# Output tiles 0 and 3 of the first batch pair computed as one group of seven products, with the output-weight sums in another order

## The chip, the core and the metric

The kernel runs on one core of a Trainium2 chip, as one program. The time is the device time of one execution in microseconds (us). A core has five engines that are used here: TensorE (PE; PEld is its weight load), VectorE (DVE), ScalarE (ACT), GpSimd (POOL) and SyncE (SP, which here only starts transfers). Each runs its own list of instructions in order, and they wait for one another through semaphores.

## What is computed

Eight batches of twelve heads, 448 positions and 64 elements go through an attention with a sigmoid in place of the softmax, and the result (3584 tokens of 768) through a gated feed-forward block:

```python
scores = scale * np.matmul(q, k.transpose(0, 1, 3, 2)) - np.log(S)
attn = 1.0 / (1.0 + np.exp(-scores))
x = np.matmul(attn, v)                  # heads side by side: 3584 x 768
g = x @ w_gate                          # 768 x 1536
out = (g * sigmoid(g) * (x @ w_val)) @ w_out      # 1536 x 768
```

## The kernel before

**Tiling.** Work goes in four pairs of batches (`pb` 0 to 3, batches 2·pb and 2·pb+1). The hidden layer has 1536 columns, in twelve blocks `f` of 128. For a batch `b` and a block `f`, `ffn1` (matmuls on line 314) multiplies x by the gate and value weights, twelve matmuls of 448 columns. Its gate follows: a sigmoid on ACT (line 334) and two products on DVE (336, 340), the last of which writes `hT`, the hidden block. Blocks 0 to 5 of pair 2 and all of pair 3 (`FAST`) are computed by `double` instead (matmuls on line 437, evictions by ACT on line 447 and DVE on line 460 and after), which takes two blocks of both batches at once with seven products instead of eight. Pair 2 runs its `ffn1` blocks 6 to 11 first and its `double` units after them.

**Output.** The 896 tokens of a pair are seven output tiles of 128 tokens (`m` 0 to 6). There are two ways to compute them:

- `ffn2` (matmuls on line 675) does one tile alone: twelve blocks by two halves of 384 columns, 24 matmuls. ACT evicts the first half (line 690) and DVE the second (line 689).
- `ffn2_group(pb, g)` (line 599) does tiles g and g+3 together, as a 2 by 2 block product with seven products of six matmuls instead of eight, 42 in place of 48. The products run in the order 1, 2, 6, 5, 7, 3, 4 and use the two banks of one PSUM tile in turn: 1, 6, 7 and 4 go to bank 0, and 2, 5 and 3 to bank 1. Before the next product may write or add to a bank, what is in it has been read by DVE (`snap`, line 610, and `put`, line 616), or for the first product by ACT (line 623) where the argument `act` is set.

The group needs sums. `make_sums` (line 532) forms sums of hidden blocks on DVE. `w_sum(s, kind)` (line 498) forms sums of the output weights, once for the whole kernel: eight DVE operations of 128 by 1152, for two halves `s` of the blocks and four kinds. Kind 2 is made from kind 3 and kind 4 from kind 2. Product 6 uses kind 2, product 5 kind 1, product 7 kind 3 and product 4 kind 4; products 1, 2 and 3 use the plain weights.

**PSUM.** It is a ring of four tiles of two banks each. Every user (`Banked`) takes the next of the four, in turn: one for each scores tile, each P·V result, each `ffn1` unit, each `ffn2` and each group. So a user always writes over the tile of the user four places before it, bank by bank, and has to wait until each bank has been read there.

**Order.** A list `units` holds the feed-forward work in order, each with an estimated duration (`FU1` 2.26 for an `ffn1`, `FU2` 3.9 for an `ffn2`, `FU3` 6.83 for a group); sums have 0. The attention is cut into `visits` of three or four score tiles (scores on line 240, their sigmoid on ACT line 259 or 256), and P·V of a finished head group (line 273, copies on DVE lines 288 and 293, or ACT line 301) follows in a later visit. Every visit has a due time, read off the line of points `PACE` over the estimated time. A loop adds up the durations of the units and puts a visit ahead of the first unit whose start is past the due time:

```python
    PACE = ((2 * NJ, FIRST + 3.5), (3 * NJ, FIRST + 41.5), (3 * NJ + 2, FIRST + 60.5), (6 * NJ, f1_end[B - 5] - 1.0), (NQ, f1_end[B - 3] - 5.0))
```

`f1_end[b]` is the estimated end of batch b's `ffn1` blocks, and contains the durations of the output units of earlier pairs. So the estimates of the first pair's output units also set where later visits go. The P·V of the last visit is done after the next `ffn1` unit; if the next unit is a `double`, it is done right ahead of that.

**First pair's output before the change.** In the list it was: all hidden sums; `ffn2` of tile 6; `w_sum` (0,3) (0,2) (0,1) (0,4); `ffn2` of tile 0; `w_sum` (1,3) (1,2) (1,1); `ffn2` of tile 3; group 1 (tiles 1 and 4), during which `w_sum` (1,4) is made; group 2 (tiles 2 and 5). The attention visits lie between them.

Of the kernel before, what the change touches and what calls it, by code (L numbers as in the profile page):

```python
# [20 lines left out]
def kernel(  # L21
# [22 lines left out]
    LAST = B // 2 - 1  # L44
# [99 lines left out]
    def half_of(a):  # L144
        return a.rearrange("p a b s -> p (a b s)").bitcast(FP16)
# [212 lines left out]
    def fast_w(s, kind, i=None):  # L358

        js = slice(0, JT) if i is None else slice(i, i + 1)  # L360
        b11, b21 = wg16[s][:, 0::2][:, js], wg16[s][:, 1::2][:, js]
        b12, b22 = wv16[s][:, 0::2][:, js], wv16[s][:, 1::2][:, js]
        if (s, kind) not in gT:
            n = JT * FW * 128
            at = {3: 0, 2: 1, 4: 2}.get(kind)
            if kind == 1:
                t = wv16[s][:, 0::2]
            elif s == 0:
                t = half_of(stg_a)[:, at * n:(at + 1) * n]
            elif s == 1 and kind == 3:  # L370
                t = half_of(ramp_a)[:, 8 * FW * hw:8 * FW * hw + n]
            elif s == 1:
                t = pt_f[:, (at - 1) * n:at * n]
            elif s == 2:
                t = pt_f[:, (at + 2) * n:(at + 3) * n]
            else:
                t = osp.tile([128, DM], FP32, tag="osb", name=f"g{kind}").bitcast(FP16)[:, :n]
            gT[(s, kind)] = t if kind == 1 else t.rearrange("p (j n) -> p j n", j=JT)
        t = gT[(s, kind)][:, js]
        a, b, op = {  # L380
            3: (b22, b12, SUB), 1: (b12, b11, SUB), 2: (b22, gT.get((s, 1), gT[(s, kind)])[:, js], SUB),
            4: (b21, gT.get((s, 2), gT[(s, kind)])[:, js], SUB),
        }[kind]
        (V if i is None else G).tensor_tensor(out=t, in0=a, in1=b, op=op)
# [104 lines left out]
    def w_sum(s, kind):  # L489

        b11, b12 = wo16[2 * s][:, :, :hw], wo16[2 * s][:, :, hw:]
        b21, b22 = wo16[2 * s + 1][:, :, :hw], wo16[2 * s + 1][:, :, hw:]
        t = half_of(ramp_a)[:, len(wT) * FW * hw:(len(wT) + 1) * FW * hw].rearrange("p (f n) -> p f n", f=FW)
        wT[(kind, s)] = t
        a, b, op = {
            3: (b22, b12, SUB), 2: (wT.get((3, s)), b11, ADD), 1: (b12, b11, SUB), 4: (b21, wT.get((2, s)), SUB),
        }[kind]
        nc.vector.tensor_tensor(out=t, in0=a, in1=b, op=op)
# [158 lines left out]
        store((nc.sync, nc.scalar), *rows[1], oe, lo)  # L657

    def ffn2_groups(pb, gs, extra=()):
        gens = [ffn2_group(pb, g, len(gs) > 1) for g in gs]  # L660
        extra = list(extra)
        while gens:
            gens = [g for g in gens if next(g, g) is not g]
            if extra:
                extra.pop(0)()
# [30 lines left out]
    FU1, FU2, FU3, FU4 = 2.26, 3.9, 6.83, 7.85  # L696
# [3 lines left out]
    for pb in range(B // 2):  # L700
        for b in (2 * pb, 2 * pb + 1):
            f1_start[b] = tt
            for f in range(NF):
                if f not in FAST.get(pb, ()):
                    if b or f > 2:
                        units.append((FU1, ffn1, (b, f)))
                    tt += FU1
            f1_end[b] = tt
        for f in FAST.get(pb, ())[::2]:
            extra = {  # L710
                (LAST - 1, 0): ((0, 4), (1, 2)), (LAST - 1, 2): ((1, 4),), (LAST, 0): ((3, 3), (3, 1)), (LAST, 2): ((3, 2), (3, 4)),
            }.get((pb, f), ())
            units.append((FU4, double, (pb, (f, f + 1), [lambda a=a: fast_w(*a) for a in extra])))
            tt += FU4
        o_units = [(0.0, make_sums, (99,))]
        if pb < LAST - 1:
            o_units.append((FU2, ffn2, (pb, C - 1)))
        if pb == 0:

            ts = [(0.0, w_sum, (s, kind)) for s in range(2) for kind in (3, 2, 1, 4)]  # L720
            o_units += ts[:4] + [(FU2, ffn2, (pb, 0))] + ts[4:7] + [(FU2, ffn2, (pb, 3))]
        ex = {(0, 1): (lambda: None, lambda: w_sum(1, 4)), (LAST - 1, 0): (keep_rest,)}
        gs = {0: ((1,), (2,)), LAST - 1: ((0, 1), (2,)), LAST: ((0, 1), (3,), (2,))}.get(pb, ((0,), (1,), (2,)))
        for g in gs:
            o_units.append((FU3 * len(g), ffn2_groups, (pb, g, ex.get((pb, g[0]), ()))))
        units += o_units
        tt += sum(u[0] for u in o_units)
# [142 lines left out]
    early = [tile_of(0), tile_of(2)]  # L870
# [126 lines left out]
```

## Time and profile before

| | us |
|---|---|
| median of 4 runs | 404.38 |
| lowest and highest | 403.76, 405.43 |
| the profiled execution, its own time | 404.66 |
| its span, first to last instruction | 402.9 |

| engine | busy us | share of the span |
|---|---|---|
| PE | 391.5 | 97% |
| DVE | 269.5 | 67% |
| ACT | 230.3 | 57% |
| POOL | 104.9 | 26% |

The span is the time between the first and the last instruction on the core; 1.76 us of the execution's time lie around it. The granted clock of TensorE was 0.998 of full speed. In a timeline row, the columns are the start, the length, the engine, the line and operation, what is written and read (without buffer numbers), and in brackets the engine's idle time before it with what ended it; rows of the same line that follow one another are merged and counted (x3). In the chain of waits, each row is a start, a length, an engine and a line: the work that the end of the program goes back to.

### The profile page before, as it was taken

The page shows a single profiled execution, that of the slowest core. Times are in us where ns is not written, and L with a number is a line of the kernel's source. Part 1 is how long each engine was busy: PE and PEld are TensorE (multiplying, and loading weights), DVE is VectorE, ACT ScalarE, POOL GpSimd, SP SyncE. Part 2 cuts the span into 40 slices and gives each one's busy share as a digit, 9 for nine tenths or more (in the row PEclk, how much of TensorE's full clock was granted, in tenths as well). Part 3 has the DMA queues.
Part 4 walks back from the last instruction along what each step waited for, and adds up shares of the span by engine and source line. Part 5 has one row for each costly group of instructions (what it writes and reads, how often), then busy time and mean ns, then how long its engine had stood idle before and what let it go on. Part 6 is the DMA issues. An engine that isn't in the chain of part 4 may idle for free.

```text
span 402.9 us, 8032 instructions
## 1 busy us (share of the span) xinstructions
PE 391.5 (97%) x3134; PEld 203.9 (51%) x3134; DVE 269.5 (67%) x509; ACT 230.3 (57%) x369; POOL 104.9 (26%) x146
## 2 busy tenths in 40 slices
PE   7799999999999999999999999999999999999995
PEld 3344544545555444444455554444555655555663
DVE  2637657779765555567774556788877578778753
ACT  5965885744344777777773447776654055756000
POOL 4528031333121232321310210000006970010700
PEclk9999999999999999999999999999999999999999
DMA  8999989999859998778716598000000520000055
GB/s 273 245 248 253 245 187 232 174 167 218 150 160 261 215 234 218 163 159 161 161 23 130 165 260 135 2 2 0 3 0 2 157 80 0 1 2 1 2 164 149
DMA packets 65286, 54.39 MB, mean 135 GB/s; under 512 B 35744, under 2 KB 61440, under 8 KB 65248
## 3 DMA queue, kind: packets, MB, share of 16 engines
q1 hardware_dynamic: 49744, 38.22, 38.5%
q0 software_dynamic: 15072, 15.34, 22.7%
q8 instruction: 24, 0.39, 0.4%
q10 hardware_dynamic: 432, 0.33, 0.3%
q14 instruction: 14, 0.11, 0.1%
HBM read 47.19 MB, written 11.01 MB: 144 GB/s over the span
## 4 chain that ended last, share of the span: by engine, by line
PE 93%; DVE 3%; ACT 2%; issue 1%; DVEq 0%; ACTq 0%
PE ps_D L314 33%; PE ps_D L599 20%; PE ps_D L437 18%; PE ps_D L240 8%; PE ps_D L273 8%; PE ps_D L675 4%; ACT pt_a L259 2%; PE ps_D L769 1%; PE ps_D L210 1%; DVE S L532 1%; DVE t L336 1%; DVE T L216 0%; ACT s L334 0%; DVE hT L340 0%; DVE xT L293 0%
## 5 line engine op out<-in xcount | busy, mean ns | idle before, releaser
L259 ACT ACTIVATE pt_a<-ps_D 128x896 f16<-128x896 f32 x148 | 127.1, 919 | 55.5 <-PE ps_D L240 50.1
L314 PE MATMUL ps_D<-xT,wg 128*128 128x448 f16 x360 | 79.4, 353 | 0.6 <-DVE t L336 0.5
L314 PE MATMUL ps_D<-xT,wv 128*128 128x448 f16 x360 | 78.9, 352 | 0.0
L191 POOL CAST c<-stg_a 128x896 bf16<-128x896 f32 x40 | 37.1, 937 | 132.8 <-DMA stg_a<-in_q_dram 116.9
L336 DVE TENSOR_TENSOR t<-ps_D,s 128x448 f16<-128x448 f32 x60 | 37.4, 623 | 43.0 <-ACT s L334 42.0
L314 PEld LDWEIGHTS <-wg 128*128 128x128 f16 x360 | 32.3, 98 | 39.4 <-issue 13.6
L314 PEld LDWEIGHTS <-wv 128*128 128x128 f16 x360 | 35.1, 98 | 33.0 <-issue 0.4
L334 ACT ACTIVATE s<-ps_D 128x448 f16<-128x448 f32 x60 | 33.1, 551 | 26.5 <-PE ps_D L314 26.5
L240 PE MATMUL ps_D<-T,T 64*64 64x448 bf16 x644 | 44.2, 357 | 2.2 <-DVE T L216 1.2
L447 ACT ACTIVATE snap<-ps_D 128x448 f32<-128x448 f32 x54 | 28.0, 541 | 26.7 <-PE ps_D L437 25.1
L340 DVE SCALAR_TENSOR_TENSOR hT<-ps_D,t 128x448 f16<-128x448 f32 x60 | 37.5, 625 | 6.3
L273 PE MATMUL ps_D<-pt_a,v 64*64 64x448 f16 x672 | 36.0, 350 | 1.3 <-DVE hT L340 0.7
L610 DVE TENSOR_SCALAR osb<-ps_D 128x384 f32<-128x384 f32 x43 | 23.9, 557 | 18.6 <-PE ps_D L599 17.9
L599 PEld LDWEIGHTS <-S 128*128 128x128 f16 x264 | 25.8, 98 | 17.1
L599 PE MATMUL ps_D<-ramp_a,S 128*128 128x384 f16 x198 | 33.6, 326 | 0.0
L616 DVE SCALAR_TENSOR_TENSOR osb<-ps_D,osb 128x384 f32<-128x384 f32 x36 | 19.9, 556 | 13.8 <-PE ps_D L599 13.8
L240 PEld LDWEIGHTS <-T 64*64 64x64 bf16 x644 | 14.9, 105 | 24.5 <-issue 17.9
L599 PEld LDWEIGHTS <-hT 128*128 128x128 f16 x204 | 19.6, 98 | 14.5 <-issue 1.8
L273 PEld LDWEIGHTS <-v 64*64 64x64 f16 x672 | 19.5, 107 | 14.2 <-issue 1.7
L288 DVE CAST xT<-ps_D 128x448 f16<-128x448 f32 x21 | 13.1, 623 | 19.3 <-PE ps_D L273 17.5
L293 DVE CAST xT<-ps_D 64x448 f16<-64x448 f32 x37 | 23.0, 622 | 0.8
L437 PE MATMUL ps_D<-xS,wv 128*128 128x448 f16 x108 | 23.4, 352 | 0.0
(110 smaller groups left out, 443.5 us busy)
## 6 DMA issues: line engine op xcount, KB each, us to landing
out_dram<-osb SPq DMA_DIRECT2D x52, 192.0 KB, 3.2
stg_a<-in_q_dram SPq DMA_DIRECT2D x18, 448.0 KB, 5.1
stg_a<-in_k_dram SPq DMA_DIRECT2D x18, 448.0 KB, 5.6
v<-in_v_dram POOLq DMA_DIRECT2D x24, 224.0 KB, 5.9
wg<-in_moe_w_gate_dram POOLq DMA_DIRECT2D x4, 576.0 KB, 12.0
wv<-in_moe_w_val_dram POOLq DMA_DIRECT2D x4, 576.0 KB, 13.1
wo<-in_moe_w_out_dram POOLq DMA_DIRECT2D x4, 576.0 KB, 9.7
stg_a<-in_q_dram POOLq DMA_DIRECT2D x3, 448.0 KB, 14.0
```

Source lines behind the costliest of these rows:

```text
L191: eng.tensor_copy(out=t.rearrange("p c h d -> p h c d"), in_=st.rearrange("p h (c d) -> p h c d", c=C))
L240: nc.tensor.matmul(out=sc[w * 64:(w + 1) * 64, h2, :S], lhsT=kt[r, w * 64:(w + 1) * 64], rhs=qt[r, :, w * 64:(w + 1) * 64], start=True, st ...
L259: nc.scalar.activation(out=pt, in_=sc[:, :, :S], func=SIGM, bias=sbias, scale=qkscale)
L273: nc.tensor.matmul(out=P[g:g + 64, h2, :S], lhsT=vt[r, h2, c * D:(c + 1) * D], rhs=pt[r, h2, :], start=(c == 0), stop=(c == C - 1),)
L314: nc.tensor.matmul(out=D.t[:, i, :S], lhsT=(wg16, wv16)[i][f // FW][:, pr, cs], rhs=xT[(b, pr)], start=(pr == 0), stop=(pr == NP - 1),),
L334: D.read(nc.scalar.activation(out=s16, in_=D.t[:, 0, :S], func=SIGM), 0)
L336: D.read(nc.vector.tensor_tensor(out=t1, in0=D.t[:, 0, :S], in1=s16, op=MULT), 0)
L340: nc.vector.scalar_tensor_tensor(out=hT[(b // 2, f)][:, b % 2, :], in0=D.t[:, 1, :S], scalar=hsc(b // 2), in1=t1, op0=MULT, op1=MULT),
L437: nc.tensor.matmul(out=D.t[:, bank, :S], lhsT=W(f, j), rhs=X(j), start=(start and j == 0), stop=(stop and j == JT - 1), skip_group_check=True,
L447: D.read(nc.scalar.mul(out=o, in_=D.t[:, bank, :S], mul=scale), bank)
L599: nc.tensor.matmul(out=D.t[:, bank, :hw], lhsT=l, rhs=B_(i), start=(first and i == 0), stop=(i == HF - 1), skip_group_check=True,),
L610: nc.vector.tensor_scalar(out=o, in0=D.t[:, bank, :hw], scalar1=1.0 / hsc(pb), scalar2=None, op0=MULT), bank
```

## The change

Tiles 0 and 3 of pair 0 become group 0, `ffn2_group(0, 0)`, with the first product read by ACT. Of the sums of the output weights, four now stand ahead of tile 6's `ffn2`: (0,3) (0,2) (1,3) (1,2). Two, (0,1) and (1,1), stand between that and group 0. The two of kind 4 are made inside group 0, after its third and its fourth step (product 6 and product 5). Group 1 no longer makes a sum. The estimated duration of the first pair's output falls from 3·3.9 + 2·6.83 = 25.36 to 3.9 + 3·6.83 = 24.39.

```diff
     def ffn2_groups(pb, gs, extra=()):
-        gens = [ffn2_group(pb, g, len(gs) > 1) for g in gs]
+        gens = [ffn2_group(pb, g, len(gs) > 1 or (pb, g) == (0, 0)) for g in gs]
...
         if pb < LAST - 1:
             o_units.append((FU2, ffn2, (pb, C - 1)))
         if pb == 0:
-
-            ts = [(0.0, w_sum, (s, kind)) for s in range(2) for kind in (3, 2, 1, 4)]
-            o_units += ts[:4] + [(FU2, ffn2, (pb, 0))] + ts[4:7] + [(FU2, ffn2, (pb, 3))]
-        ex = {(0, 1): (lambda: None, lambda: w_sum(1, 4)), (LAST - 1, 0): (keep_rest,)}
-        gs = {0: ((1,), (2,)), LAST - 1: ((0, 1), (2,)), LAST: ((0, 1), (3,), (2,))}.get(pb, ((0,), (1,), (2,)))
+            early = [(0.0, w_sum, a) for a in ((0, 3), (0, 2), (1, 3), (1, 2), (0, 1), (1, 1))]
+            o_units[1:1] = early[:4]
+            o_units += early[4:]
+        skip = lambda: None
+        ex = {
+            (0, 0): (skip, skip, lambda: w_sum(0, 4), lambda: w_sum(1, 4)), (LAST - 1, 0): (keep_rest,),
+        }
+        gs = {LAST - 1: ((0, 1), (2,)), LAST: ((0, 1), (3,), (2,))}.get(pb, ((0,), (1,), (2,)))
```

## The prediction

> **What bounds the kernel.** I read the page's busy shares and chain first, then the chain in order of time around the output of pair 0 and around the last visit, then DVE's and ACT's timelines there.
>
> ```profile
> PE 391.5 (97%) x3134; PEld 203.9 (51%) x3134; DVE 269.5 (67%) x509; ACT 230.3 (57%) x369; POOL 104.9 (26%) x146
> PE 93%; DVE 3%; ACT 2%; issue 1%; DVEq 0%; ACTq 0%
> ```
>
> ```profile
> 98.10 3.90 PE ps_D L675 x24
> 102.00 0.69 PE ps_D L240 x12
> 102.70 7.91 PE ps_D L675 x48
> 110.60 0.50 PE ps_D L240 x8
> ...
> 272.38 0.69 PE ps_D L240 x12
> 273.07 2.38 PE ps_D L314 x12
> 275.44 1.45 PE ps_D L273 x28
> 276.89 2.38 PE ps_D L314 x12
> 279.27 23.84 PE ps_D L437 x126
> ```
>
> From 95 us on PE is back to back: each piece starts where the last one ends, and no other engine stands between. So a matmul less is worth its time, and a wait that PE gets is lost in full, since nothing later has idle time to give back.
>
> ```profile
> 98.65 0.62 DVE L340 SCALAR_TENSOR_TENSOR hT<-ps_D,t 128x448 f16<-128x448 f32 x1
> ...
> 101.98 0.62 DVE L532 TENSOR_TENSOR S<-hT,S 128x384 f16<-128x384 f16 x2
> 102.51 0.55 DVE L689 TENSOR_SCALAR osb<-ps_D 128x384 f32<-128x384 f32 x1
> 102.98 0.75 DVE L498 TENSOR_TENSOR ramp_a<-wo,wo 128x1152 f16<-128x1152 f16 x1
> 103.76 0.76 DVE L498 TENSOR_TENSOR ramp_a<-ramp_a,wo 128x1152 f16<-128x1152 f16 x1
> 104.44 0.75 DVE L498 TENSOR_TENSOR ramp_a<-wo 128x1152 f16<-128x1152 f16 x1
> 105.11 0.75 DVE L498 TENSOR_TENSOR ramp_a<-wo,ramp_a 128x1152 f16<-128x1152 f16 x1
> ```
>
> DVE isn't idle between 98.65 and 105.86. Tile 6's eviction (L689) comes as soon as the hidden sums (L532) are done, and the weight sums (L498) follow it.
>
> ```profile
> 102.37 2.54 ACT L259 ACTIVATE pt_a<-ps_D 128x896 f16<-128x896 f32 x3
> ...
> 272.74 2.54 ACT L259 ACTIVATE pt_a<-ps_D 128x896 f16<-128x896 f32 x3 [0.72 <-PE ps_D L240]
> 272.78 0.62 DVE L340 SCALAR_TENSOR_TENSOR hT<-ps_D,t 128x448 f16<-128x448 f32 x1
> ```
>
> The three sigmoids of a visit take ACT until 2.54 us after the first starts, 0.36 us after the visit's scores began at 272.38.
>
> **The matmuls.** 48 matmuls in 7.91 us are 0.165 us each; the chain has a whole group of 42 at 112.81 in 6.93. Six fewer: **-0.98**.
>
> **The moved sums and the ring.** Ring users after the change are tile 6's `ffn2`, three score tiles, then group 0: group 0 writes tile 6's PSUM tile. Its product 1 (bank 0) waits for ACT's L690, done by 102.37, which costs nothing. Product 2 (bank 1) waits for DVE's L689. This now stands behind four L498. Hidden sums end at 101.98+0.62 = 102.60; the four take about what they take before, 105.86-102.98 = 2.88, so to 105.5; L689 ends about 106.08. Product 1 runs 102.70 to 103.68, product 2 from 106.12: a wait of **2.44**. Behind L689 on DVE are everything that releases the group's banks, and on SP tile 6's store with the transposes of head group 10 and a load behind it, which go 3 us later than at 104.39; head group 10 isn't read before 127, so that is covered.
>
> The rest of the group, in steps of 0.98, an eviction of 0.56 that can start some 0.2 after its product's last matmul has issued, and L498 of 0.75:
> - DVE does (0,1) and (1,1) to 107.43, the put of product 2 to 107.99. PE does product 2 to 107.10 and 6 to 108.07 (ACT's eviction of product 1 follows the sigmoids, 104.91+0.5 = 105.4; that would be a wait of 0.75 if the first weren't there). Product 5 needs the put: just in time.
> - DVE evicts 6 by 108.83, sums (0,4) by 109.52, evicts 5 by 110.06, sums (1,4) by 110.75, puts 7 by 111.3. PE does 5 to 109.05, 7 to 110.02, waits 0.06, 3 to 111.08, waits for the put of 7: **0.26**; product 4 ends at 112.32.
>
> Group 0 thus ends at 112.32 where 48 matmuls ended at 110.60: **+1.72** in all, with the 0.98 gained counted. The following visit's third score tile takes the group's PSUM tile at 114.1, after the last eviction (113.1).
>
> Bounds. Two hidden sums there took 1.07 and 1.11 where the others take 0.35, beside POOL casts at 99.12 and 100.26. If those casts land elsewhere, DVE is 1.47 earlier; product 2 starts at 104.65, but product 5 then waits for its put, to 106.6, and the group ends near 110.75, **+0.2**. If as many other sums are hit as well it is 1.47 worse, **+3.2**. POOL has no work between 102.0 and 110.6, so I keep 1.7.
>
> The Trainium skill's page "TensorE: Matmul & The Clock Gate" (Part 1) bears on such a wait. In the trace, PE was busy for only 2.78 of the 4.00 us from 8 to 12 with the clock at 1.00. By the page, an idle window of about 3.4 us halves the clock for about as long; 2.44 is below it. By the rule the sum stays as it is; were the wait just above the window it would be an estimated 1.7 dearer. No row here shows such an idle window.
>
> **The estimate and the visits.** The first pair's estimate falls by 0.97, and so does that of `f1_end[5]`, the last point of `PACE`. In the built order the visits keep their places up to the end of pair 1; from there each comes one `ffn1` unit, or one output unit, later. In most places that only swaps blocks of PE work: I go through DVE's queue in pair 2 and the copies of P·V end just before the next visit's first score tile needs them (by 272.2 where PE comes at 272.3). That is cost nothing, with 0.1 of cover.
>
> At the end it does cost. The last visit now stands right before `double`. Its P·V has no `ffn1` unit ahead of it, and needs the visit's last sigmoid. In the times of before, with scores from 272.38: P·V's PSUM tile is that of the preceding `ffn1`, free when L340 ends at 273.40 (there it may be 0.1 later, with one more hidden sum ahead). Sixteen of its matmuls run to 274.2; the last sigmoid ends at 275.28, the last four matmuls (0.19) at 275.5. `double` starts there, 3.13 after the scores. The two units that stood between are done earlier, at 4.64 for two in a row (chain: 4.64 or 4.65). Sum 3.13+4.64 = 7.77; before, 279.27-272.38 = 6.89: **+0.88**. The bounds: 0.1 more or less by the DVE order, and 0.3 less if the first sigmoid starts sooner. `double`'s own evictions are later against it by about 0.3, as the activation table load now follows the last sigmoid; the next use of that bank comes 0.7 after them, so nothing.
>
> **Sum.** 1.72 + 0.88 = 2.6. On the profiled execution: 404.66 + 2.6 = 407.3; it was 0.28 over the median 404.38, so the median goes to **407.0**.
>
> **Rivals.**
> - *Both as worked out*: 406.1 to 408.0 (group 0 from +1.2 to +2.6, end from +0.5 to +1.0). 66%.
> - *The saving stands (not slower)*: L689 gets through early, because DVE has reached the sums sooner, and group 0 runs without a wait. Price: -0.98, with the end's +0.88 then 404.3, without it 403.4. It decides where L689 ends by 103.7, before product 2; this needs the four L498 (2.88) to start at 100.3, where DVE still has four hidden sums to do. The 67% of DVE speaks for it, the rows above against it. 10%, nearly all of it within 0.3%.
> - *The end costs nothing*: +1.7 alone, 406.1; if the last sigmoids come before P·V's matmuls do. Against: ACT has 2.54 for them, PE 1.5 of work. 14%, from 405.7 to 406.4.
> - *More*: a store or a transpose behind L689 on SP becomes late, or DVE is held up by casts in group 0 also, and PE waits 1.5 to 2 more: 408.0 to 409. For it: only 0.1 of cover in pair 2. 10%.
>
> 0.3% is 1.2 us, about what a measurement of this kernel can tell from no change. Faster by over that has 3% (it needs -1.2, more than all six matmuls), same 9%, slower 88%. The range leaves out most of the second rival and half of the last: 405.5 to 408.6.
>
> **What would show it.** In the chain of the changed kernel, DVE L498 and L689 between the scores at 102.0 and group 0's matmuls; L689 near 105.5; group 0 (L599 x42) over about 9.6 us instead of 6.9. At the end ACT L259 in the chain, between the scores and P·V, right ahead of L437; the other groups at 6.93. I am wrong if product 2 starts right after product 1, if the group's 42 matmuls take 7 us, or if P·V before L437 takes 1.3 as elsewhere.

## The result

The changed kernel takes 405.98 us, the median of 50 runs (405.20 to 411.34), where the kernel before takes 404.54 on the same chips (74 runs). The ratio is 1.0036, with a 95% interval of 1.0025 to 1.0046: 1.0 to 1.9 us slower. The forecast of 407.0 had the sign right and was 1.0 us too high; its range held the time. The profiled execution of after took 405.97 (span 404.2), 1.31 more than that of before.

From the page of after, the busy shares and the chain's shares:

```profile
PE 393.2 (97%) x3128; PEld 204.9 (51%) x3128; DVE 272.5 (67%) x514; ACT 229.5 (57%) x367; POOL 105.7 (26%) x146
PE 30%; ACT 0%; DVE 0%; issue 0%; DVEq 0%
```

PE has six matmuls less, and DVE is busy for 3.0 more. The chain gives PE 30% only because it could not be followed back beyond 279.23 us. So stages are compared here by their start times in the timelines instead. Three marks serve for every kernel: the scores of the visit ahead of the output that is in question (L240 x12, at 101.93 in before) to the scores behind it; from those to the first matmul of the first `double` after the last visit (L437); from there to the last eviction (L610). In before's timelines these are

```profile
101.93 0.76 PE L240 MATMUL ps_D<-T,T 64*64 64x448 bf16 x12
110.53 0.57 PE L240 MATMUL ps_D<-T,T 64*64 64x448 bf16 x8
279.11 2.43 PE L437 MATMUL ps_D<-xT,wg 128*128 128x448 f16 x12
398.66 0.56 DVE L610 TENSOR_SCALAR stg_a<-ps_D 128x384 f32<-128x384 f32 x1 [0.49 <-PE ps_D L599]
```

and in after's the last two (the first two are the first and the last row of group 0's timeline further down)

```profile
280.41 2.44 PE L437 MATMUL ps_D<-xT,wg 128*128 128x448 f16 x12
399.97 0.56 DVE L610 TENSOR_SCALAR stg_a<-ps_D 128x384 f32<-128x384 f32 x1 [0.49 <-PE ps_D L599]
```

| kernel | scores to scores | to `double` | to the last eviction | sum |
|---|---|---|---|---|
| before | 8.60 | 168.58 | 119.55 | 296.73 |
| after | 8.59 | 170.04 | 119.56 | 298.19 |

The sum rises by 1.46; the first scores came 0.15 sooner in after's execution, which leaves the 1.31. So the group of seven products takes as long as the two tiles alone took, though it has six matmuls less, and the whole loss lies at the end.

Group 0, in PE's and DVE's timelines of after (start, length, engine, line, operation; the brackets tell what ended the idle time):

```profile
101.78 0.76 PE L240 MATMUL ps_D<-T,T 64*64 64x448 bf16 x12
102.48 1.15 PE L599 MATMUL ps_D<-wo,hT 128*128 128x384 f16 x6
104.28 1.14 PE L599 MATMUL ps_D<-wo,hT 128*128 128x384 f16 x6 [0.66 <-DVE osb L689]
105.25 3.09 PE L599 MATMUL ps_D<-ramp_a,S 128*128 128x384 f16 x18
108.18 1.14 PE L599 MATMUL ps_D<-wo,S 128*128 128x384 f16 x6
109.30 1.14 PE L599 MATMUL ps_D<-ramp_a,hT 128*128 128x384 f16 x6
110.37 0.57 PE L240 MATMUL ps_D<-T,T 64*64 64x448 bf16 x8
```

```profile
99.94 0.36 DVE L532 TENSOR_TENSOR S<-S,hT 128x384 f16<-128x384 f16 x1
100.22 0.62 DVE L532 TENSOR_TENSOR S<-hT,S 128x384 f16<-128x384 f16 x2
100.76 0.75 DVE L498 TENSOR_TENSOR ramp_a<-wo,wo 128x1152 f16<-128x1152 f16 x1
101.54 0.76 DVE L498 TENSOR_TENSOR ramp_a<-ramp_a,wo 128x1152 f16<-128x1152 f16 x1
102.22 0.75 DVE L498 TENSOR_TENSOR ramp_a<-wo,wo 128x1152 f16<-128x1152 f16 x1
103.00 0.76 DVE L498 TENSOR_TENSOR ramp_a<-ramp_a,wo 128x1152 f16<-128x1152 f16 x1
103.68 0.55 DVE L689 TENSOR_SCALAR osb<-ps_D 128x384 f32<-128x384 f32 x1
```

Product 2 waits for tile 6's eviction L689, and this is behind the four L498, as forecast. But the wait is 0.66 and not 2.44, as the hidden sums (L532) take 0.36 and less here and the four weight sums begin at 100.76. The forecast had counted its 2.44 from start to start, less the step of 0.98; counted like that the wait is 0.82 (104.28 - 102.48 - 0.98).

The end, in after's timeline:

```profile
274.45 0.75 DVE L384 TENSOR_TENSOR stg_a<-wv 128x1152 f16<-128x1152 f16 x1
275.12 0.62 DVE L288 CAST stg_a<-ps_D 128x448 f16<-128x448 f32 x1
275.77 1.26 DVE L293 CAST stg_a<-ps_D 64x448 f16<-64x448 f32 x2
277.08 0.76 PE L240 MATMUL ps_D<-T,T 64*64 64x448 bf16 x12 [0.32 <-DVE stg_a L293]
277.51 2.54 ACT L259 ACTIVATE pt_a<-ps_D 128x896 f16<-128x896 f32 x3 [1.10 <-PE ps_D L240]
278.46 1.33 PE L273 MATMUL ps_D<-pt_a,v 64*64 64x448 f16 x24 [0.62 <-DVE hT L340]
280.10 0.38 PE L273 MATMUL ps_D<-pt_a,v 64*64 64x448 f16 x4 [0.30 <-ACT pt_a L259]
```

Two losses are to be seen. P·V waits 0.62 for its PSUM tile (L340), and its last four matmuls then wait 0.30 for the last sigmoid (L259), the loss that was forecast. And the visit's scores (L240) wait 0.32 for the copies of the P·V before (L293), which DVE does only behind a weight sum for `double` (L384). That one had been counted at nothing.

### The profile page after: what moved, and what is told of

Its sections match the earlier page's. It is cut to its first block, busy times and chain, and to the rows that moved or that the text cites. A ratio compares the mean times of both kernels' runs of the same rounds, so it can differ in the third digit from the quotient of the medians.

```text
span 404.2 us, 8021 instructions
## 1 busy us (share of the span) xinstructions
PE 393.2 (97%) x3128; PEld 204.9 (51%) x3128; DVE 272.5 (67%) x514; ACT 229.5 (57%) x367; POOL 105.7 (26%) x146
## 5 line engine op out<-in xcount | busy, mean ns | idle before, releaser
L259 ACT ACTIVATE pt_a<-ps_D 128x896 f16<-128x896 f32 x148 | 127.2, 917 | 61.4 <-PE ps_D L240 56.0
L336 DVE TENSOR_TENSOR t<-ps_D,s 128x448 f16<-128x448 f32 x60 | 37.4, 623 | 42.3 <-ACT s L334 41.4
L334 ACT ACTIVATE s<-ps_D 128x448 f16<-128x448 f32 x60 | 33.0, 550 | 27.5 <-PE ps_D L314 27.5
L240 PE MATMUL ps_D<-T,T 64*64 64x448 bf16 x644 | 44.3, 360 | 1.7 <-DVE T L216 0.6
L340 DVE SCALAR_TENSOR_TENSOR hT<-ps_D,t 128x448 f16<-128x448 f32 x60 | 37.5, 625 | 6.3
L610 DVE TENSOR_SCALAR osb<-ps_D 128x384 f32<-128x384 f32 x46 | 25.6, 557 | 19.4 <-PE ps_D L599 19.1
L599 PEld LDWEIGHTS <-S 128*128 128x128 f16 x288 | 28.2, 98 | 18.6
L599 PE MATMUL ps_D<-ramp_a,S 128*128 128x384 f16 x216 | 36.7, 326 | 0.0
L616 DVE SCALAR_TENSOR_TENSOR osb<-ps_D,osb 128x384 f32<-128x384 f32 x39 | 21.6, 556 | 13.8 <-PE ps_D L599 13.7
L599 PEld LDWEIGHTS <-hT 128*128 128x128 f16 x222 | 21.2, 98 | 16.8 <-issue 3.2
L240 PEld LDWEIGHTS <-T 64*64 64x64 bf16 x644 | 15.2, 106 | 24.1 <-issue 17.7
L599 PE MATMUL ps_D<-wo,hT 128*128 128x384 f16 x144 | 25.2, 326 | 0.7 <-DVE osb L689 0.7
L293 DVE CAST xT<-ps_D 64x448 f16<-64x448 f32 x37 | 23.0, 622 | 0.8
```

Of the source, the lines that this page charges most:

```text
L240: nc.tensor.matmul(out=sc[w * 64:(w + 1) * 64, h2, :S], lhsT=kt[r, w * 64:(w + 1) * 64], rhs=qt[r, :, w * 64:(w + 1) * 64], start=True, st ...
L259: nc.scalar.activation(out=pt, in_=sc[:, :, :S], func=SIGM, bias=sbias, scale=qkscale)
L334: D.read(nc.scalar.activation(out=s16, in_=D.t[:, 0, :S], func=SIGM), 0)
L336: D.read(nc.vector.tensor_tensor(out=t1, in0=D.t[:, 0, :S], in1=s16, op=MULT), 0)
L340: nc.vector.scalar_tensor_tensor(out=hT[(b // 2, f)][:, b % 2, :], in0=D.t[:, 1, :S], scalar=hsc(b // 2), in1=t1, op0=MULT, op1=MULT),
L599: nc.tensor.matmul(out=D.t[:, bank, :hw], lhsT=l, rhs=B_(i), start=(first and i == 0), stop=(i == HF - 1), skip_group_check=True,),
```

## The experiments

The theory has two parts. In group 0 a wait behind the weight sums eats what the six matmuls save. At the end the last P·V stands unprotected behind its sigmoids, because the estimate moved the visits. The rivals are named with each run. A stage below is one of those in the table above; where a kernel has lines more or fewer than after, its line numbers are a few higher or lower. Each time is a median where nothing else is said, and its ratio is to executions of before beside it (medians 404.49, 404.58 or 404.23).

**Visits kept.** Group 0 is entered in the list with the estimate of the two tiles it replaces, so every visit stands where it stood before.

```diff
-            o_units.append((FU3 * len(g), ffn2_groups, (pb, g, ex.get((pb, g[0]), ()))))
+            o_units.append((2 * FU2 if (pb, g) == (0, (0,)) else FU3 * len(g), ffn2_groups, (pb, g, ex.get((pb, g[0]), ()))))
```

> The changed kernel, with group 0 entered in the plan at 7.8 us as the two single tiles were, so that every attention visit stands where it stood before. Theory (the loss is the last visit's, group 0 pays about as much as it gains): the end goes back to 6.9 us from the last scores to the first double, and the whole is 1.4 us under the changed kernel, within 0.3 us of before (404.3 to 404.8). Rival (the loss is group 0's wait for tile 6's eviction): it stays at 406.0, since group 0 is the same.

Measured: 404.78 against 404.49, ratio 1.0006 (0.9978 to 1.0035). Scores to scores 8.59, to `double` 168.57: the end's loss is gone to the last hundredth, and group 0 is left, which costs and brings nothing.

**Visits only.** The other half, in the kernel before: its second tile is entered with the lower estimate and nothing else is changed.

```diff
-            o_units += ts[:4] + [(FU2, ffn2, (pb, 0))] + ts[4:7] + [(FU2, ffn2, (pb, 3))]
+            o_units += ts[:4] + [(FU2, ffn2, (pb, 0))] + ts[4:7] + [(FU3 - FU2, ffn2, (pb, 3))]
```

> The kernel before, with only the plan's estimate of the first pair's output lowered by 0.97 us, so that the visits stand where the change puts them; no group 0, sums as before. Theory: the end alone costs it 1.3 to 1.4 us, 405.8 to 406.0, with a wait of P.V for the last sigmoid and 0.3 us of the last scores for DVE's copies. Rival (group 0): 404.5, like before. A third: if the moved visits cost something between pair 1 and the end too, it is above 406.2.

Measured: 406.42, ratio 1.0045 (1.0025 to 1.0065). Scores to scores 8.60, to `double` 170.05, that is 1.47 more than before, with the same two waits. The median lies above the 406.2 of the third case, but in the profiled execution (405.75) the moved visits cost nothing more than these 1.47, and the interval reaches from 405.5 to 407.1. An estimate that no engine executes makes this kernel as slow as the whole change does.

**POOL's casts put on the sums.** Group 0 lost less than forecast because the sums ran undisturbed. In before, hidden sums of 0.35 took 1.07 and 1.11 beside POOL's casts at 99.12 and 100.26; in after these casts were at 96.58 and 97.70 and met no sum. Here POOL's next conversions of q and k are held back until the last hidden block (`hT`) is written.

```diff
+    def hold_for(src):
+        G.tensor_copy(out=held[:, :1], in_=src())
...
+    late = (lambda: hT[(0, NF - 1)][:, 1, S - 1:])
     for n in range(8, NQ - 2):
-        plan[(n, 4)] = ((ready, n + 2), (load_v, n + 2)) + ((load_qk, n + 4),) * (n + 4 < NQ)
+        plan[(n, 4)] = ((hold_for, late),) * (n == 9) + ((ready, n + 2), (load_v, n + 2)) + ((load_qk, n + 4),) * (n + 4 < NQ)
```

> The changed kernel, with one small GpSimd copy that makes the two casts of head group 11 wait until the last hidden block of the first pair is written, so that they run beside the hidden sums. Theory (what the casts meet decides the wait): the sums there are held up by 1.4 to 1.9 us in all, tile 6's eviction ends that much later, product 2 waits 2 us or more instead of 0.66, and the whole is 1.3 to 1.7 us over the changed kernel, 407.3 to 407.7. Rival (casts and sums don't meet, the long sums in the profile of before had another cause): 406.0.

Measured: 407.17, ratio 1.0069 (1.0044 to 1.0094). The casts came later than meant, as q was loaded only by 101.19; they missed the hidden sums and met a weight sum. POOL's row and DVE's:

```profile
101.19 0.93 POOL L191 CAST c<-stg_a 128x896 bf16<-128x896 f32 x1 [2.14 <-DMA stg_a<-in_q_dram]
101.28 1.45 DVE L498 TENSOR_TENSOR ramp_a<-ramp_a,wo 128x1152 f16<-128x1152 f16 x1
```

One L498 takes 1.45 instead of 0.76, PE's wait for L689 is 1.48 instead of 0.66 (2 or more had been expected), and scores to scores 9.42 instead of 8.59. The lengthened sum makes 0.69 of the 0.83; the rest is that the weight sums began 0.89 before the scores, where in after they began 1.02 before them. So a lengthened sum reaches PE in full. The median is 1.2 above that of after; in the profiled execution the last stage is 0.55 longer too (see the last section).

**The casts put behind the sums.** The same hold, on the last sum of the output weights: `late = (lambda: wT[(4, 1)][:, FW - 1, hw - 1:])`.

> The changed kernel, with the same two casts held back until the last sum of the output weights is made, behind group 0's sums. Theory: group 0 is as in the profile of the changed kernel, where the casts came ahead of the sums by chance (product 2 waits 0.6 to 0.7 us), so 405.8 to 406.1; if in most runs of the changed kernel the casts do meet the sums, it is below the changed kernel by up to 1 us. Rival (later casts make head group 11's transposes late): above 406.3, with PE waiting for a transpose near 137 us.

Measured: 406.22, ratio 1.0040 (1.0022 to 1.0057). The casts run at 108.13, behind all sums; the wait is 0.66 and the stage 8.59, as in after, and the median is 0.24 above after's. So the usual execution of after seems to be one in which the casts do not meet the sums. The other profiled executions with this group 0 and with free casts fit that: visits kept and the three runs on the end further down show a wait of 0.66 to 0.75, and in only one of these five executions, after's included, was one of the sums longer (0.44). But the casts can meet the sums here as well: in the next run they came at 97.87 and did.

**More work of POOL on the sums.** Four copies of 128 by 512 are added on POOL, held until the last hidden block is written.

```diff
+    def four_casts(n):
+        G.tensor_copy(out=held[:, :1], in_=hT[(0, NF - 1)][:, 1, S - 1:])
+        for _ in range(4):
+            G.tensor_copy(out=warm, in_=wo16[0].rearrange("p f n -> p (f n)")[:, :512])
...
-        plan[(n, 4)] = ((ready, n + 2), (load_v, n + 2)) + ((load_qk, n + 4),) * (n + 4 < NQ)
+        plan[(n, 4)] = ((ready, n + 2),) + ((four_casts, n),) * (n == 9) + ((load_v, n + 2),) + ((load_qk, n + 4),) * (n + 4 < NQ)
```

> The changed kernel, with four GpSimd copies of 128 by 512 that have no use, started when the last hidden block of the first pair is written, so that GpSimd's work meets VectorE's sums whenever the transfers come. Theory (whether GpSimd's work meets the sums decides group 0's wait, as in my working, which took this from the profile of before): 1.2 to 2.2 us on the hidden and weight sums, and the stage from the scores before group 0 to those behind it is longer than 8.59 us by as much, 9.8 to 10.8; the time 407.2 to 408.2. Rival (VectorE isn't held up by GpSimd's copies): 8.6 us and 406.0.

Measured: 406.97, ratio 1.0080 (1.0047 to 1.0112). The profiled execution, with a span of 408.2, lies well above this median, so its stage of 12.80 is that of a bad case. In it, five of the last six hidden sums and one weight sum were held up, the first two by the usual casts (97.87 to 99.85) and the others by the added copies (from 100.04), and the wait and what follows it read, in PE's timeline:

```profile
106.22 1.18 PE L599 MATMUL ps_D<-wo,hT 128*128 128x384 f16 x6 [3.33 <-DVE osb L689]
107.20 4.76 PE L599 MATMUL ps_D<-ramp_a,S 128*128 128x384 f16 x18
```

and in the table of windows (length, busy us and instructions of PE, PEld, DVE, ACT and POOL, granted clock, DMA share, GB/s):

```profile
104.00:108.00 4.00, 1.78 (x9) 1.02 (x9) 3.97 (x7) 0.50 (x2) 0.00 (x0) 0.90 0.63 92
108.00:112.00 4.00, 4.00 (x19) 2.00 (x17) 2.25 (x5) 0.00 (x0) 0.00 (x0) 0.68 0.99 193
```

The wait grew by 2.67 over after's 0.66, and the 18 matmuls behind it took 4.76 instead of 3.09, at a granted clock of 0.68 to 0.90. So the wait that the forecast named as the bad case exists, and it comes with a lower clock besides. The median is just under the 407.2 to 408.2 that were expected.

**Tile 6's and two group evictions on ACT.** With the visits kept: tile 6's second half and the evictions of products 6 and 5 go to ACT, the first product's goes back to DVE, and the two sums of kind 1 move into the group.

```diff
+            if (pb, g, half) == (0, 0, 1):
+                D.read(nc.scalar.mul(out=o, in_=D.t[:, bank, :hw], mul=1.0 / hsc(pb)), bank)
+                return
...
-        gens = [ffn2_group(pb, g, len(gs) > 1 or (pb, g) == (0, 0)) for g in gs]
+        gens = [ffn2_group(pb, g, len(gs) > 1) for g in gs]
...
-                V.tensor_scalar(out=o, in0=i, scalar1=by, scalar2=None, op0=MULT) if half else
+                V.tensor_scalar(out=o, in0=i, scalar1=by, scalar2=None, op0=MULT) if half and (pb, m) != (0, C - 1) else
...
-            o_units += early[4:]
...
-            (0, 0): (skip, skip, lambda: w_sum(0, 4), lambda: w_sum(1, 4)), (LAST - 1, 0): (keep_rest,),
+            (0, 0): (skip, lambda: (w_sum(0, 1), w_sum(1, 1)), lambda: w_sum(0, 4), lambda: w_sum(1, 4)), (LAST - 1, 0): (keep_rest,),
```

> Group 0 with the visits kept, and evictions moved: tile 6's second half and the two evictions of group 0 that only copy (after products 6 and 5) go to ScalarE, which is idle behind its sigmoids, the one after product 1 goes to VectorE, and the two kind 1 sums come behind the put of product 2. Theory (what is left of group 0's wait is VectorE's load of sums and evictions between 99 and 110 us): product 2 doesn't wait for tile 6, the group takes 7.4 to 7.6 us instead of 7.9, and the whole is 0.3 to 0.5 us under the visits-kept kernel, 404.3 to 404.5. Rival (the wait only moves on): the same 7.9 us, with the wait at product 5.

Measured: 404.23 against before's 404.58, ratio 0.9985 (0.9964 to 1.0006). The wait for L689 is gone and the stage is 8.31, 0.28 less than in after. Not more, because product 5 then waits for a weight sum, as the waits of PE show (us in total, times, longest):

```profile
PE ps_D L599 <- DVE ramp_a L498: 0.3, 1, 0.3
```

**Hidden sums of kind 4 later as well.** The same, with the hidden sums of kind 4, which only product 3, the last but one, reads, moved out of DVE's queue ahead of the group, to the group's third step.

```diff
+    def first_sums():
+        sumq.sort(key=lambda s: s[3] % 3 if s[3] < 4 else 3)
+        make_sums(sum(s[3] < 4 for s in sumq))
...
-        o_units = [(0.0, make_sums, (99,))]
+        o_units = [(0.0, make_sums, (99,)) if pb else (0.0, first_sums, ())]
...
+            (0, 0): (skip, lambda: (w_sum(0, 1), w_sum(1, 1)), lambda: (make_sums(99), w_sum(0, 4)), lambda: w_sum(1, 4)), (LAST - 1, 0): (keep_rest,),
```

> The kernel with group 0's evictions moved to ScalarE and the visits kept, and the two hidden sums of kind 4, which only product 3 needs, made after the kind 1 weight sums instead of ahead of all weight sums. Theory (VectorE's queue sets group 0's wait): the kind 1 weight sums come 0.6 us earlier, product 5's wait of 0.5 us goes, the group takes 6.9 to 7.2 us, and the whole is 0.4 us under the kernel without this, 403.7 to 404.0, and 0.5 to 0.8 us under before. Rival (another wait takes its place, at product 3 or 4, for the sums that are now later): 7.5 us for the group, no difference.

Measured: 404.00 against before's 404.23, ratio 0.9992 (0.9977 to 1.0007). The stage is 8.31 again, with the same wait of 0.34. DVE reached the group earlier but stood idle before its evictions; the two sums of kind 1 come in its program behind the put of product 2, which waits for PE, and so they start at 104.23 whatever is cleared ahead of it. DVE's order was the limit here, not the amount of its work. No run with the weight sums in place brings the stage below 8.31.

**No weight sums.** With the visits kept; it leaves out the eight sums of the output weights and multiplies plain weights in their place, so what it computes is not the output wanted.

```diff
-        nc.vector.tensor_tensor(out=t, in0=a, in1=b, op=op)
...
-            return lambda i: wT[(kind, i // FW)][:, i % FW, :]
+            return lambda i: wo16[2 * (i // FW)][:, i % FW, :hw]
```

> Group 0 with the visits kept, with the eight sums of the output weights left out and plain weights multiplied in their place in all groups; the matmuls and their number stay. Theory: without the sums VectorE is free for tile 6's eviction, group 0 runs in 6.9 us like the other groups, and the six matmuls less become visible, 0.9 to 1.0 us under the visits-kept kernel: 403.6 to 403.9. Rival (a group that follows a single tile waits for its PSUM tile anyway, or for ScalarE's eviction behind the three sigmoids): product 6 waits some 0.75 us, 7.6 us for the group, 404.5.

Measured: 404.07 against 404.58, ratio 0.9987 (0.9975 to 0.9999). The stage is 8.37, not 7.6. DVE is no longer in PE's way, but ACT is: product 6 waits for the first product's eviction, which ACT (here L622) does only behind the visit's three sigmoids. The row of the waits:

```profile
PE ps_D L598 <- ACT osb L622: 0.6, 1, 0.6
```

and ACT's timeline:

```profile
101.92 2.54 ACT L259 ACTIVATE pt_a<-ps_D 128x896 f16<-128x896 f32 x3
104.32 0.51 ACT L622 ACTIVATE osb<-ps_D 128x384 f32<-128x384 f32 x1
```

The forecast had this second wait (0.75, "if the first weren't there").

**No weight sums, and the first product read by DVE.** The same, and `len(gs) > 1 or (pb, g) == (0, 0)` becomes `len(gs) > 1`.

> The kernel without the output-weight sums and with the visits of before, and the first product of group 0 read by DVE in place of ACT. Leaves out the eight sums of the output weights (plain weights are multiplied instead). Theory (two covers hide the six matmuls: DVE's queue at product 2, and ACT's sigmoids ahead of the first product's eviction): with both gone nothing holds group 0 and the stage from scores to scores takes 7.6 us instead of 8.37, that is 0.97 less than before. Rival (the banks themselves, two of them with an eviction each between seven products, hold the group): DVE's evictions make PE wait between products and the stage stays above 8.0.

One execution, whose time is no use here: PE had lost 2.31 us to a wait that ended at 88.92, ahead of everything that differs. The stage takes 7.62 (105.99 to 113.61), as the theory said, and the chain shows the group without a gap:

```profile
106.06 0.69 PE ps_D L240 x12
106.75 6.93 PE ps_D L598 x42
```

So the six matmuls are worth 0.97 against after's stage, 0.98 against before's, once both waits are gone, and the two banks alone do not hold the group up.

**Last P·V inside `double`.** After, with the last P·V put behind the first two products of `double`, which need none of these sigmoids.

```diff
+        if pend and fn is double:
+            args[2][:0] = [lambda n=n: pv(n)() for n in pend]
+            pend = []
```

> The changed kernel, with the last P.V put behind the first two products of the first double instead of ahead of it; nothing else moves. Theory (P.V waits for the visit's last sigmoid): that wait, 1.1 us, goes, and the 0.3 us of the last scores for VectorE's copies stays: 404.8 to 405.0. Rival (the end's loss comes from the copies or the table load): 405.7 to 406.0.

Measured: 407.49 against 404.58, ratio 1.0072 (1.0047 to 1.0097), the wrong way. P·V no longer waits for its sigmoid, but its copies now stand on DVE ahead of what `double` waits for, in the waits of PE:

```profile
PE ps_D L437 <- DVE v L473: 1.3, 1, 1.3
```

DVE's first operation of `double` (L460) is late besides. It starts 4.16 after `double` does, in after 2.04: it needs ACT's eviction of `double`'s first product, and ACT gets to that only behind the visit's sigmoids and its table load (1.28). No run separates the two. From the scores ahead of the whole to the last eviction it is 0.83 more than after. The loss only changed its place.

**The same with sums for `double` made earlier.** The L384 that sat ahead of the copies is carried one block earlier, and so is the one before it.

```diff
-                (-2, h + 5, xs2[6:9]), (-1, h, xs2[9:]), (-1, h + 2, w2[2:3]), (-1, h + 3, w2[3:4]),
-                (-1, h + 4, w2[4:]),
+                (-2, h + 5, xs2[6:9]), (-1, h, xs2[9:]), (-1, h + 2, w2[2:4]), (-1, h + 3, w2[4:]),
```

> As the kernel with the last P.V in the first double, and the gate-weight sum of block 10 made one unit earlier, so that VectorE reaches the copies of the last but one P.V 0.7 us sooner. Theory: the last scores don't wait for the copies any more, 0.3 us less again: 404.4 to 404.7, and from the last scores on the end is as short as before the change. Rival (the copies' delay comes from elsewhere): as the kernel without it.

Measured: 406.62, ratio 1.0053 (1.0030 to 1.0076). The last scores wait no longer, which brings 0.39 between the scores behind group 0 and `double`; the 1.3 at L473 stays, so 404.4 to 404.7 is missed as well.

**Only those sums earlier.** After, with the second edit alone, to split the end's loss in two.

> The changed kernel, with the weight sums that the blocks of pair 2 carry for double's units put one block earlier, so that the last of them (L384) is no longer ahead of the copies of P·V (L288, L293) on DVE. Theory (0.3 to 0.4 of the end's loss of 1.46 us is these copies, the rest is the wait for the last sigmoid): the wait of 0.32 at the last scores for L293 is gone, the wait of 0.30 for L259 ahead of P·V's last four matmuls stays, and from group 0's end to the first double it takes 169.65 to 169.75 us in place of 170.04. Rival (what the last visit's scores win, its sigmoids or double give back): the wait is gone, but a new one stands behind it, at L314 two blocks earlier or at L437, and that stretch and the stretch of double together come down by less than 0.1.

One execution: 404.94, with 404.57 for before beside it. To `double` takes 169.67 (expected 169.65 to 169.75), `double` to the last eviction stays at 119.56. In PE's timeline:

```profile
276.03 0.76 PE L240 MATMUL ps_D<-T,T 64*64 64x448 bf16 x12
277.19 1.44 PE L273 MATMUL ps_D<-pt_a,v 64*64 64x448 f16 x24 [0.39 <-DVE hT L340]
279.05 0.38 PE L273 MATMUL ps_D<-pt_a,v 64*64 64x448 f16 x4 [0.43 <-ACT pt_a L259]
```

The scores wait for nothing; P·V's two waits stay, and the last one is for the last sigmoid. So the end's 1.46 is 0.37 from the copies and 1.09 from P·V right ahead of `double`. This rests on one execution, but the stage is steady: in the five executions with the visits moved and the end as in after it took 170.04 to 170.06.

Which version is best? None that forms all its sums beats the kernel before by more than its interval. The changed group with the visits kept and the evictions on ACT is level with it (0.9985, 0.9964 to 1.0006) and takes, by the medians, 1.75 us less than the change as it was made.

## Why the prediction was right, and where not

- **The sign and both mechanisms** were right. The "visits kept" and "visits only" runs show that the two parts are separate and that they add up.
- **The number** owes something to luck. The sum was 1.72 + 0.88 = 2.6, the stages show -0.01 + 1.46 = 1.45: the larger term was nothing, and the smaller one was the whole loss. With the end at 0.88 the time would have been about 405.4 (404.54 - 0.01 + 0.88), just below the range.
- **The matmuls, -0.98.** Right: 0.98 from before's stage (8.60 to 7.62), when nothing covers them. In the changed kernel the waits take all of it.
- **Group 0, +1.72: mis-sized.** It measured -0.01. The wait of 2.44 for L689 was 0.82 by the same count (0.66 idle), since the four weight sums began 1.0 before the visit's scores instead of 0.6 behind them. The failed step is "Hidden sums end at 101.98+0.62 = 102.60", taken from one profiled execution in which POOL's casts had met two of the hidden sums. The forecast saw this (its lower bound of +0.2 is this case) and chose the other end because before's row showed it. The "casts behind the sums" run, at 8.59, shows the group with sums that nothing holds up, and its median, 0.24 from after's, suggests that this end is the usual one. The lower bound itself had product 5 waiting for its put; it did not wait, as the put was done at 106.07 and product 5 was due about 106.2 (105.25 + 0.98). Of the waits of 0.06 and 0.26 further on, the first did not come and the second was 0.14 (108.18 to 109.30, less 0.98). So 0.82 and 0.14 took what the six matmuls had saved. By the forecast's own signs group 0 lies in between: 7.9 (102.48 to 110.37), where 9.6 was expected and 7 would have refuted it.
- **The end, +0.88: mis-sized.** It measured 1.46. Of this, 1.09 is P·V right ahead of `double`, waiting for the sigmoid at last. Its missing 0.2 is in P·V's last four matmuls: 0.04 from the sigmoid's end to their start and 0.31 to L437, where 0.22 had been allowed for both; and the first sigmoid comes 0.43 after the scores, where the forecast had 0.36, a start from the chain set against one from the timeline. The other 0.37 is the step "That is cost nothing, with 0.1 of cover": the copies did not end 0.1 before the scores needed them but made them wait for 0.32. The walk through DVE's queue came out 0.4 too early, and the run with only those sums earlier shows what decides there: with the L384 right ahead of the copies gone, the scores wait for nothing.
- **The rivals.** "The end costs nothing" fell: the end is the whole loss, though its 406.1 is close to what was measured and its range, 405.7 to 406.4, holds it: the right number for the wrong reason. "The saving stands" fell, as L689 ended 2.45 after the scores had begun (104.23) and not by 1.7; but the wait of 0.82 is nearer to none than to the 2.44 that was taken. "More" named the 0.1 of cover in pair 2 as its weak point, and that did give way, at 0.37 rather than 1.5 to 2.
- **The likeliest case's own range**, 406.1 to 408.0, just missed 405.98: its lower end for group 0, +1.2, left out the case of undisturbed sums.
- **The reading "PE is back to back" from 95 us on** has two exceptions: before's chain goes over ACT's L334 and DVE's L336 at 131.61 and 171.62, where PE waits 0.22 and 0.28. It did not matter, as the stage to `double` took 168.57 to 168.59 in every run that kept the visits.
- **The Trainium skill's clock rule**, "TensorE: Matmul & The Clock Gate" (Part 1), was weighed with an idle window of about 3.4 and an estimate of 1.7 for a wait just above it, and no row of before showed one. The runs show the price, but not the window. Behind a wait of 3.33 (more work on POOL) the matmuls were 1.67 late, at clocks of 0.90 and 0.68. Behind a wait of only 2.31 (no weight sums and DVE first; rows in the last section) the next twelve were 1.69 late, and from 88 to 92 the clock was 0.64. After waits of 0.66, 1.48 and 1.93 the windows show 1.00. So that 2.44 would leave the sum as it is was not safe: a wait of that length might have cost an estimated 1.7 more, and the measurement decides here, not the window.

## What to carry to other kernels

Six matmuls less are worth their time only if the engines that free the banks can follow: before a product is moved up to a visit, go through DVE's and ACT's queues there, as each had a wait ready when the other's was taken away. A planner's estimate is part of the kernel. Changing one moves work far away, so enter it so that the order stays, or cost the new order at its tightest place. Where one profile shows an operation at three times its usual length, find out what else ran there before building a sum on it, because the next execution may not have it.

## What was not expected of the hardware

- What a DVE operation with two inputs in SBUF costs depends on when the loads land that POOL then converts. The 128 by 384 sum took 0.35 alone and about 1.0 beside a cast of 0.93; the 128 by 1152 sum 0.76 alone and 1.45. DVE's evictions from PSUM stayed at 0.54 to 0.56, beside a cast as well (with the casts put on the sums, L689 took 0.55 at 104.11, and a cast ran from 103.70 to 104.98). The runs agree with the lock on the port pair shared by DVE and GpSimd that the Trainium skill describes in "SBUF — State Buffer" (Who interferes with whom).
- The same thing sets much of the scatter between executions. In the run without sums and with DVE's first eviction, four casts of POOL in a row met a hidden sum of 0.36 ahead of the first output tile:

```profile
84.44 3.69 POOL L191 CAST c<-stg_a 128x896 bf16<-128x896 f32 x4
84.45 2.88 DVE L531 TENSOR_TENSOR S<-hT,S 128x384 f16<-128x384 f16 x1
88.92 2.25 PE L314 MATMUL ps_D<-xT,wg 128*128 128x448 f16 x6 [2.31 <-DVE t L336]
90.96 2.08 PE L314 MATMUL ps_D<-xT,wv 128*128 128x448 f16 x6
```

  PE waited 2.31, and its next two sets of six matmuls took 2.25 and 2.08 in place of 1.30 each. In the "visits kept" run such a sum took 2.51 and PE waited 1.93, but there the next six took 1.30 again; in after's profiled execution the four casts came 1.3 later, and PE lost nothing there. In all, the scores ahead of group 0 began between 100.9 and 106.0 in the profiled executions, so stages had to be compared instead of single times.
- In five executions (visits kept, the three runs that hold POOL back or give it more work, hidden sums later) the last stage took 0.55 more, each with a wait of 0.4 at L437 for L473. Ahead of it on DVE stands a sum for `double` (L384), and POOL forms sums of the same line at that time. In the "visits kept" run:

```profile
327.83 2.91 DVE L384 TENSOR_TENSOR g<-wv 128x1152 f16<-128x1152 f16 x1
327.46 2.66 POOL L384 TENSOR_TENSOR pt_a<-wg,pt_a 128x384 f16<-128x384 f16 x3
```

  In all five DVE's sum took 2.90 or 2.91 and POOL's three 2.65 or 2.66; in the other nine executions DVE's took 1.15 to 1.18, and POOL's three 3.68 to 3.70. So here too one of the two engines holds the other up. What decides which of them stays open; it did not go with any one edit.
